# Counting a verdict with a small matmul in the tail of a fused GateLoop and gated feed-forward kernel

## The chip, the cores and the metric

The kernel runs on one core of one Trainium2 chip. The metric is the device time of one execution in microseconds (us). Times given for "runs" are of ordinary executions; the profile is of one further execution.

## The reference

Two stages follow one another. The first is a gated linear attention with a complex decay per step, the second a feed-forward layer with the gate h·cos(h).

```python
# q, k, v, a_re, a_im: (4, 8, 768, 48), float32
mag = sqrt(a_re**2 + a_im**2)
a_re, a_im = (a * minimum(mag, 0.999) / (mag + 1e-6) for a in (a_re, a_im))
for t in range(768):
    S_re, S_im = (a_re[t] * S_re - a_im[t] * S_im + outer(k[t], v[t]),
                  a_re[t] * S_im + a_im[t] * S_re)
    y[t] = q[t] @ S_re
x = y as (4 * 768, 8 * 48)
h = x @ w_in                # (3072, 384) @ (384, 2048)
out = (h * cos(h)) @ w_out  # (3072, 2048) @ (2048, 384)
```

## The kernel before

The kernel holds two programs. `fast_path` makes assumptions on the data: that the decays over a chunk do not underflow, that the weights (which arrive as 64-bit floats) are not too small, and that h stays in the range in which the sine table serves. `general_path` assumes none of this. The fast path always runs; as it goes it collects evidence in three small tiles, `least` (96 x 16, flags 1 or 0 from the decays), `odd` (128 x 41, from the weights) and `wide` (128 x 96, sums of squares of h). Near the end the generator `verdict` makes one number of them, `flag`. Every engine reads `flag` and branches: if it is 1, the whole general path runs; if not, only the last store of the fast path is issued, which stands behind the branch so that a bad result can still be replaced.

The fast path takes the 3072 rows in twelve groups of two chunks of 128 rows. In the feed-forward stage of groups 2 to 11, `mm1_sums` makes h in PSUM, `gate_sine` and `gate_product` make the gate, and `products` makes the second matmul as seven products of a 2 x 2 scheme in place of eight, each of two parts of 8 steps. `seventh(g, p, part)` does one part of one product. The order of the products is 0, 1, 3, 2, 5, 4, 6: products 0, 3, 5 (and 6, but for the last group) accumulate in one PSUM tile `sum`, which is copied out after each to the quarter of the output that it makes up at that point; products 1, 2, 4 (and 6 of the last group) have a PSUM tile `op` of their own and are added to those quarters by VectorE. In the last group (`NG - 1`) the upper right quarter `c12` lies in a tile of its own, `rest`, and its store, `late["store"]`, is the one behind the branch. It is issued by ScalarE; all other stores of the output are issued by SyncE.

The order of instructions is written out by hand. `weave` merges lists of steps by fractions of a stretch. In the last stretch it merges the fourteen parts of the products with three calls of `judged`, each of which runs `verdict` up to its next `yield`. The call `behind(a, b)` keeps instruction a after b on the same engine without a semaphore; `late` holds the instructions that others are put behind. TensorE's instructions are chained in the order in which they are written. `matmul` records all of TensorE's products under line 687, and the wrappers `vector` and `scalar` record most of the other engines' instructions under lines 676 and 707, so that in the profile groups are told apart by their tiles.

`verdict` in the kernel before: it reduces `least` to `low` (96 x 1), `odd` to `even` and `wide` to `most` (128 x 1 each), compares the latter two and multiplies them. As these lie across partitions, it brings them into one row through memory: `low` and `even` go to a scratch line `line_d` (lines 1620 and 1622), which is read back as 1 x 224 into a tile of tag `Q` (line 1624). `bad` is the minimum of that row (line 1627), and `flag` tells whether it is below 0.5 (line 1630). `values_load_multi_w_load_instructions` (line 1632) makes each engine load `flag`, and line 1644 branches. ScalarE's load is put behind the last copy of `sum` written so far (`late["scalar"]`), VectorE's ahead of the last addition, TensorE's behind a late product.

Of the kernel before, what the change touches and what calls it, by code (L numbers as in the profile page):

```python
# [11 lines left out]
F32 = mybir.dt.float32  # L12
# [7 lines left out]
ALU = mybir.AluOpType  # L20
AX = mybir.AxisListType
# [466 lines left out]
def fast_path(ctx, tc, q, k, v, a_re, a_im, moe_w_in, moe_w_out, out, least, odd, wide,  # L488
# [7 lines left out]
    nc = tc.nc  # L496
    B, H, S, D = q.shape
    DM, DF = moe_w_in.shape
    C = 128
# [3 lines left out]
    NG = N // G  # L503
    D2 = 2 * D
# [17 lines left out]
    pa = ctx.enter_context(tc.tile_pool(name="pa", bufs=5, space=PSUM))  # L522
# [11 lines left out]
    late = {}  # L534
# [8 lines left out]
    def behind(ins, other):  # L543
        tc.add_manual_dep(ins.ins, other.ins.name, mybir.DependencyInfo(
            mybir.DependencyClass.NoSync, mybir.DependencyReason.DATA))
# [9 lines left out]
    def scalar_tile(value, name):  # L555
        t = consts.tile([C, 1], F32, name=name)
        nc.vector.memset(t, value)
        return t
# [33 lines left out]
    one_b = scalar_tile(1.0, "one_b")  # L592
# [91 lines left out]
    vector, scalar = Ordered(nc.vector, "vector"), Ordered(nc.scalar, "scalar")  # L684

    def matmul(out, **kw):
        chain(nc.tensor.matmul(out, **kw), "tensor")  # L687
# [430 lines left out]
    PLAIN, HJ, E2 = 2, NJ // 2, DM // 2  # L1118
# [33 lines left out]
    scale = 1.0 / (in_scale * out_scale)  # L1152

    def left(g, name, j):
        if name[0] == "s":
            return X[g]["mix"][j // 2][name][:, j % 2]
        half, i = int(name[2]) - 1, int(name[1]) - 1
        return X[g]["gate"][j // 2 + half * (HJ // 2)][:, j % 2, ts(i, C)]

    def seventh(g, p, part):  # L1160


        x, name = X[g], SEVEN[p]
        if p == 0 and part == 0:
            x["sum"] = pm.tile([C, E2], F32, tag="acc", name="sum", bufs=1)
            x["ot"] = [msb.tile([C, DM], F32, tag="ot", name="ot") for _ in range(G)]

        alone = g == NG - 1 and p == 6
        summed = p in (0, 3, 5, 6) and not alone
        if not summed and part == 0:  # L1170
            x["op"] = pm.tile([C, E2], F32, tag="m", name="op", bufs=2)
        ps = x["sum"] if summed else x["op"]
        for j in range(part * HJ // 2, (part + 1) * HJ // 2):
            matmul(ps, lhsT=left(g, name, j), rhs=right[name][:, j],
                   start=(j == 0 and (p == 0 or not summed)),
                   stop=(j == HJ - 1), skip_group_check=summed)
        if part == 0:
            return
        c11, c12, c21, c22 = (x["ot"][i][:, ts(half, E2)] for i in range(2) for half in range(2))
        if g == NG - 1:  # L1180
            c12 = rest
        if p in (0, 3, 5) or p == 6 and not alone:
            late["scalar"] = scalar.mul(out={0: c11, 3: c21, 5: c22, 6: c12}[p], in_=ps, mul=scale)
        if g == NG - 1 and p == 5:
            scalar.mul(out=c12, in_=ps, mul=scale)
        for part_ in {1: [c11], 2: [c21], 4: [c21, c22], 6: [c12] * alone}.get(p, []):
            added = vector.scalar_tensor_tensor(out=part_, in0=ps, scalar=scale,
                                                in1=part_, op0=ALU.mult, op1=ALU.add)
            if alone:
                behind(added, late["read DVE"])  # L1190
            late["vector"] = added
        row = g * G * C
        if g == NG - 1 and p == 1:
            behind(nc.sync.dma_start(out=out[ds(row, C), 0:E2], in_=c11), late["line"])
        elif p == 4:
            put = nc.sync.dma_start(out=out[ds(row + C, C), :], in_=x["ot"][1])
            if g == NG - 1:
                behind(put, late["read SP"])
        elif p == 6 and alone:
            late["store"] = lambda: nc.scalar.dma_start(out=out[ds(row, C), E2:DM], in_=c12)  # L1200
        elif p == 6:
            nc.sync.dma_start(out=out[ds(row, C), :], in_=x["ot"][0])

    def products(g, lo, hi):
        if g < PLAIN:
            return []
        return [lambda p=p, part=part: seventh(g, p, part)
                for p in (0, 1, 3, 2, 5, 4, 6)[lo:hi] for part in range(2)]

    def mixes(g, lo, hi):  # L1210
        return [lambda p=p: mixed(g, p) for p in range(lo, hi)] if g >= PLAIN else []
# [204 lines left out]
    even = even_steps(1, 0, G)  # L1416
# [101 lines left out]
    even = even_steps(2, 0, G)  # L1518
# [49 lines left out]
    for n in range(2, NG):  # L1568
# [5 lines left out]
              (keys(n + 1), *((0.5, 0.62) if n == PLAIN else (0.53, 0.64))),  # L1574
              (last_quarter() if n == PLAIN else [], 0.9, 1.0), (first(n), 0.56, 1.0),
              (mixes(n, 0, 2), 0.9, 1.0), (guarded(n - 1, per) if n > 3 else [], 0.1, 0.9))
    checked = verdict(late, temp)

    def judged():
        late["tensor"] = tail["tensor"]  # L1580
        next(checked, None)

    weave((mixes(NG - 1, 2, 4), 0.0, 0.1), ([judged], 0.05, 0.15),
          (products(NG - 1, 0, 7), 0.0, 1.0), ([judged], 0.58, 0.6), ([judged], 0.76, 0.8))
    assert not guards
    return late
@with_exitstack
def kernel(ctx, tc, q, k, v, a_re, a_im, moe_w_in, moe_w_out, out):

    nc = tc.nc
    D2, H = 2 * q.shape[3], q.shape[1]
    keep = ctx.enter_context(tc.tile_pool(name="keep", bufs=1))
    least = keep.tile([D2, 2 * H], F32, name="least")
    C = 128
    NG, NJ = q.shape[0] * q.shape[2] // C // 2, moe_w_out.shape[0] // C
    odd = keep.tile([C, moe_w_in.shape[0] // C * 4 + NJ + NG + 1], F32, name="odd")
    wide = keep.tile([C, NG * NJ // 2], F32, name="wide")
    rest = keep.tile([C, moe_w_out.shape[1] // 2], F32, name="rest")  # L1600
    scratch = ctx.enter_context(tc.tile_pool(name="scratch", bufs=1,
                                             space=bass.MemoryType.DRAM))

    def behind(ins, other):
        tc.add_manual_dep(ins.ins, other.ins.name, mybir.DependencyInfo(
            mybir.DependencyClass.NoSync, mybir.DependencyReason.DATA))

    def verdict(late, temp):

        low = keep.tile([D2, 1], F32, name="low")  # L1610
        nc.vector.tensor_reduce(out=low, in_=least, axis=AX.X, op=ALU.min)
        even = keep.tile([C, 1], F32, name="even")
        nc.vector.tensor_reduce(out=even, in_=odd, axis=AX.X, op=ALU.max)
        most = keep.tile([C, 1], F32, name="most")
        nc.vector.tensor_reduce(out=most, in_=wide, axis=AX.X, op=ALU.max)
        nc.vector.tensor_scalar(out=even, in0=even, scalar1=0.0, scalar2=None, op0=ALU.is_le)
        nc.vector.tensor_scalar(out=most, in0=most, scalar1=2.4, scalar2=None, op0=ALU.is_le)
        nc.vector.tensor_tensor(out=even, in0=even, in1=most, op=ALU.mult)
        line_d = scratch.tile([D2 + C], F32, name="line_d")
        behind(nc.sync.dma_start(out=line_d[0:D2], in_=low.rearrange("p o -> (p o)")),  # L1620
               late["x"])
        nc.sync.dma_start(out=line_d[D2:D2 + C], in_=even.rearrange("p o -> (p o)"))
        line = temp("Q")[0:1, 0:D2 + C]
        late["line"] = nc.sync.dma_start(out=line, in_=line_d.unsqueeze(0))
        yield
        bad = keep.tile([1, 2], F32, name="bad")
        behind(nc.vector.tensor_reduce(out=bad[:, 0:1], in_=line, axis=AX.X, op=ALU.min),
               late["vector"])
        flag = keep.tile([1, 1], I32, name="flag")
        nc.vector.tensor_scalar(out=flag, in0=bad[:, 0:1], scalar1=0.5, scalar2=None,  # L1630
                                op0=ALU.is_lt)
        reads, values = nc.values_load_multi_w_load_instructions(
            flag[0:1, 0:1], min_val=0, max_val=1,
            skip_runtime_bounds_check_because="a comparison gives 0 or 1")
        late["taken"] = values[0]
        for ins in reads:
            name = str(ins.ins.engine).split(".")[-1]
            late["read " + name] = ins
        behind(late["read Activation"], late["scalar"])
        yield  # L1640
        behind(late["read PE"], late["tensor"])

    late = fast_path(tc, q, k, v, a_re, a_im, moe_w_in, moe_w_out, out, least, odd, wide, rest, verdict)
    with tc.If(late["taken"] > 0) as taken:
        general_path(tc, q, k, v, a_re, a_im, moe_w_in, moe_w_out, out)
    with taken.Else():
        late["store"]()
# [30 lines left out]
```

## Time and profile before

| what | us |
|---|---|
| median of 3 runs | 655.76 |
| lowest and highest run | 654.2, 656.69 |
| the profiled execution | 653.01 |
| its span, first to last instruction | 651.2 |
| TensorE busy in the span | 641.0 (98%) |
| VectorE busy | 492.0 (76%) |
| ScalarE busy | 392.8 (60%) |
| last matmul ended, from the start of the span | 646.55 |

The span is what the profiler saw; the profiled execution's own time is 1.8 us longer. Busy times are sums of the durations of one engine's instructions; instructions of the queues (loads of registers, branches, semaphores, issues of transfers) are not in them, but can be listed by line. In such lists PE is TensorE's matmul, PEld its loading of weights, DVE VectorE, ACT ScalarE, SP SyncE, and a q behind the name means the engine's queue. TensorE's granted clock was 1.0 of full speed in the whole span.

### The profile page before, as it was taken

The numbers are of one execution on the slowest core, as the hardware profiler recorded it, in microseconds if no ns is written. First come the engines' busy times: TensorE is split into PE (matmuls) and PEld (weight loads), VectorE is DVE, ScalarE is ACT, GpSimd is POOL, SyncE is SP. The second block draws the span as 40 slices with busy tenths as digits, with TensorE's granted clock in tenths as the row PEclk, the third lists the DMA queues.
The fourth block names the chain that finished last, engine by engine and source line by source line (L and its number), as shares of the span: only waits on it lengthen the run. The fifth ranks groups of instructions, "written<-read, shape, count | busy, mean of one in ns | idle before, by whom it ended". The sixth has DMA issues, their size and how long they took to land.

```text
span 651.2 us, 10758 instructions
## 1 busy us (share of the span) xinstructions
PE 641.0 (98%) x4075; PEld 576.4 (89%) x4075; DVE 492.0 (76%) x799; ACT 392.8 (60%) x726; POOL 30.9 (5%) x53
## 2 busy tenths in 40 slices
PE   8999999999999999999999999999999999999997
PEld 6888877777999999899899899899899999999996
DVE  6999989888687688786787787876877878862251
ACT  7898687284583593494494485485576476433330
POOL 4010200000000000010010010000000000000000
PEclk9999999999999999999999999999999999999999
DMA  9968755727627656747738737836836843363001
GB/s 249 244 179 203 225 164 123 170 62 182 146 49 182 158 146 148 194 110 167 209 82 191 204 85 167 205 96 151 226 105 146 219 123 98 112 134 120 25 1 31
DMA packets 232920, 94.90 MB, mean 146 GB/s; under 512 B 208701, under 2 KB 221246, under 8 KB 232858
## 3 DMA queue, kind: packets, MB, share of 16 engines
q1 hardware_dynamic: 225320, 68.51, 45.3%
q0 software_dynamic: 5824, 25.50, 11.7%
q8 instruction: 34, 0.56, 0.4%
q10 hardware_dynamic: 1714, 0.11, 0.2%
q14 instruction: 28, 0.23, 0.1%
HBM read 69.28 MB, written 24.81 MB: 144 GB/s over the span
## 4 chain that ended last, share of the span: by engine, by line
PE 92%; ACT 4%; DVE 3%; DMA 0%; issue 0%; SPq 0%; DVEq 0%
PE hp L687 38%; PE op L687 18%; PE sum L687 16%; PE sc L687 6%; PE yp L687 6%; PE sp L687 4%; PE phs L687 2%; PE lgs L687 1%; ACT tan L707 1%; PE yr L687 1%; PE tp L948 1%; ACT rs L707 1%; ACT lg L707 1%; ACT L703 1%; DVE mag L676 1%; DVE atm L676 1%
## 5 line engine op out<-in xcount | busy, mean ns | idle before, releaser
L687 PE MATMUL hp<-xT,w_in 128*128 128x256 f32 (+1 forms) x1176 | 252.5, 375 | 0.0
L687 PEld LDWEIGHTS hp<-xT,w_in 128*128 128x128 f32 x1176 | 219.6, 190 | 30.2 <-issue 0.2
L707 ACT ACTIVATE gate<-hp,half_pi_b 128x512 f32<-128x512 f32 x96 | 66.0, 687 | 118.5 <-PE hp L687 118.5
L687 PE MATMUL op<-w_out,gate 128*128 128x192 f32 (+1 forms) x448 | 100.7, 374 | 0.0
L676 DVE TENSOR_TENSOR gate<-hp,gate 128x512 f32<-128x512 f32 x96 | 65.7, 684 | 45.8 <-ACT junk L676 45.7
L687 PEld LDWEIGHTS op<-w_out,gate 128*128 128x128 f32 x448 | 75.9, 190 | 16.9 <-issue 2.0
L676 ACT ACTIVATE junk<-hp 128x512 bf16<-128x512 f32 x96 | 56.7, 591 | 0.0
L687 PE MATMUL sum<-t_s,s 128*128 128x192 f32 x320 | 56.3, 329 | 0.0
L687 PEld LDWEIGHTS sum<-t_s,s 128*128 128x128 f32 x320 | 52.1, 190 | 1.5 <-issue 1.5
L676 DVE TENSOR_TENSOR atm<-sc,causal 128x512 f32<-128x512 f32 x48 | 32.9, 689 | 23.4 <-PE sc L687 23.4
L687 PEld LDWEIGHTS sc<-qT,kT 96*128 96x128 f32 x384 | 47.4, 192 | 2.3 <-issue 0.6
L687 PE MATMUL sc<-qT,kT 96*128 96x128 f32 x384 | 49.0, 276 | 0.2 <-ACT qT L676 0.2
L676 ACT ACTIVATE ot<-sum 128x192 f32<-128x192 f32 x39 | 12.6, 322 | 53.7 <-PE sum L687 53.4
L676 DVE SCALAR_TENSOR_TENSOR ot<-op,ot 128x192 f32<-128x192 f32 x40 | 13.3, 354 | 38.0 <-PE op L687 36.4
L687 PE MATMUL yp<-atm,v 128*48 128x128 f32 x352 | 33.6, 277 | 0.9 <-ACT Q L707 0.6
L703 ACT ACT_TABLE_LOAD x24 | 30.8, 1283 | 1.2 <-PEq L1662 0.7
L676 ACT COPY yT<-yp 48x512 f32<-48x512 f32 x44 | 25.3, 574 | 7.4 <-PE yp L687 7.0
L687 PE MATMUL yp<-qT,state 96*48 96x128 f32 x304 | 29.7, 272 | 0.0
L687 PE MATMUL sum<-w_out,gate 128*128 128x192 f32 x160 | 29.7, 329 | 0.0
L687 PE MATMUL sp<-v,ks 128*96 128x48 f32 x320 | 29.7, 245 | 0.0
L687 PEld LDWEIGHTS sp<-v,ks 128*96 128x96 f32 x320 | 29.6, 165 | 0.0
L676 ACT CAST tan<-phs 128x384 int32<-128x384 f32 x24 | 11.4, 480 | 29.4 <-PE phs L687 29.4
(147 smaller groups left out, 987.4 us busy)
## 6 DMA issues: line engine op xcount, KB each, us to landing
moved<-tr SPq DMA_DIRECT2D x20, 768.0 KB
raw<-in_moe_w_in_dram POOLq DMA_DIRECT2D x16, 768.0 KB, 5.1
raw<-in_moe_w_out_dram POOLq DMA_DIRECT2D x16, 768.0 KB, 4.6
kT<-moved SPq DMA_DIRECT2D x40, 192.0 KB
qT<-moved SPq DMA_DIRECT2D x10, 768.0 KB
k<-in_k_dram SPq DMA_DIRECT2D x24, 192.0 KB
q<-in_q_dram SPq DMA_DIRECT2D x24, 192.0 KB
v<-in_v_dram SPq DMA_DIRECT2D x24, 192.0 KB
```

The source lines that it names most:

```text
L676: ins = getattr(self.engine, op)(**kw)
L687: chain(nc.tensor.matmul(out, **kw), "tensor")
L703: chain(nc.scalar.preload_act_table_set(table))
L707: chain(nc.scalar.activation(func=func, **kw))
L948: chain(nc.tensor.transpose(ps[:, h], X[g][name[0] + "s"][:, x0 + h].rearrange("p a d -> p (a d)"), ident), "tensor")
```

## The change

The three factors are now 1 or 0 in each partition and are multiplied into one column `even` (the 96 values of `low` into its first 96 partitions). A matmul with `even` as weights and a column of ones as moving operand counts them into a 1 x 1 tile `good` in PSUM, and `flag` tells whether the count is below 127.5. The transfers through memory and the reduction `bad` are gone, and the first store of the last group no longer has to stand behind the transfer of the line. The second call of `judged` moves from the fraction 0.58 to 0.42, after the third product. In the last group, product 5's sum is copied to `c22` and to `c12` by VectorE in place of ScalarE, so ScalarE's last copy ahead of its branch is that of product 3.

```diff
@@ seventh
         if g == NG - 1:
             c12 = rest
-        if p in (0, 3, 5) or p == 6 and not alone:
+        if g == NG - 1 and p == 5:
+            for out_ in c22, c12:
+                vector.tensor_scalar(out=out_, in0=ps, scalar1=scale, scalar2=None, op0=ALU.mult)
+        elif p in (0, 3, 5) or p == 6 and not alone:
             late["scalar"] = scalar.mul(out={0: c11, 3: c21, 5: c22, 6: c12}[p], in_=ps, mul=scale)
-        if g == NG - 1 and p == 5:
-            scalar.mul(out=c12, in_=ps, mul=scale)
...
         if g == NG - 1 and p == 1:
-            behind(nc.sync.dma_start(out=out[ds(row, C), 0:E2], in_=c11), late["line"])
+            nc.sync.dma_start(out=out[ds(row, C), 0:E2], in_=c11)
@@ end of fast_path
-    checked = verdict(late, temp)
+    def counted(even):
+
+        ps = pa.tile([1, 1], F32, tag="a", name="good")
+        matmul(ps, lhsT=even, rhs=one_b, start=True, stop=True)
+        return ps
+
+    checked = verdict(late, counted)
...
-          (products(NG - 1, 0, 7), 0.0, 1.0), ([judged], 0.58, 0.6), ([judged], 0.76, 0.8))
+          (products(NG - 1, 0, 7), 0.0, 1.0), ([judged], 0.42, 0.44), ([judged], 0.76, 0.8))
@@ verdict
         nc.vector.tensor_tensor(out=even, in0=even, in1=most, op=ALU.mult)
-        line_d = scratch.tile([D2 + C], F32, name="line_d")
-        behind(nc.sync.dma_start(out=line_d[0:D2], in_=low.rearrange("p o -> (p o)")),
-               late["x"])
-        nc.sync.dma_start(out=line_d[D2:D2 + C], in_=even.rearrange("p o -> (p o)"))
-        line = temp("Q")[0:1, 0:D2 + C]
-        late["line"] = nc.sync.dma_start(out=line, in_=line_d.unsqueeze(0))
+        nc.vector.tensor_tensor(out=even[0:D2], in0=even[0:D2], in1=low, op=ALU.mult)
         yield
-        bad = keep.tile([1, 2], F32, name="bad")
-        behind(nc.vector.tensor_reduce(out=bad[:, 0:1], in_=line, axis=AX.X, op=ALU.min),
-               late["vector"])
+        good = counted(even)
         flag = keep.tile([1, 1], I32, name="flag")
-        nc.vector.tensor_scalar(out=flag, in0=bad[:, 0:1], scalar1=0.5, scalar2=None,
-                                op0=ALU.is_lt)
+        behind(nc.vector.tensor_scalar(out=flag, in0=good, scalar1=C - 0.5, scalar2=None,
+                                       op0=ALU.is_lt), late["vector"])
```

More of the change, by code (lines that the diff above doesn't have):

```diff
@@ L1606, in behind, with verdict @@
             mybir.DependencyClass.NoSync, mybir.DependencyReason.DATA))
-    def verdict(late, temp):
+    def verdict(late, counted):
         low = keep.tile([D2, 1], F32, name="low")
```

## The prediction

> **What bounds the kernel now.** I read the page first. TensorE is busy 98% of the 651.2 us span at a granted clock of 1.0, and the chain that ended last is 92% PE. VectorE and ScalarE stand idle for 24% and 40%, so work moved between them matters only where PE or the end waits for it. Every edit lies in the last group of rows, so the second view is the chain of waits in order of time, at its end (start us, length us, what):
>
> ```profile
> 628.33 2.60 PE sum L687 x16
> 630.93 2.60 PE op L687 x16
> 633.53 2.60 PE sum L687 x16
> 636.13 2.60 PE op L687 x16
> 638.73 2.60 PE sum L687 x16
> 641.33 5.21 PE op L687 x32
> 646.55 0.03 issue
> 646.58 0.02 DVEq L676
> 646.60 0.04 issue
> 646.64 0.36 DVE rest L676
> ```
>
> The seven products follow one another with no gap, 2.60 us for 16 matmuls or 0.163 us each. Nothing of the verdict holds PE. After the last matmul (646.55) come one VectorE addition into `rest`, ending at 647.00, and then 4.2 us that the chain does not show. Third view, the timeline of the tail, for the verdict's way through memory:
>
> ```profile
> 631.90 0.15 DVE L1618 TENSOR_TENSOR even<-even,most 128x1 f32<-128x1 f32 x1
> 632.08 0.33 SPq L1622 DMA_DIRECT2D line_d<-even  x1
> 638.54 0.25 SPq L1624 DMA_DIRECT2D Q<-line_d  x1
> 641.72 0.38 DVE L1627 TENSOR_REDUCE bad<-Q 1x1 f32<-1x224 f32 x1 [2.54 <-DMA Q<-line_d]
> 642.13 0.14 DVE L1630 TENSOR_SCALAR flag<-bad 1x1 int32<-1x1 f32 x1
> 647.03 1.17 ACTq L1200 DMA_DIRECT2D out_dram<-rest  x1
> ```
>
> The verdict takes from 632.05 (`even` done) to 642.27 (`flag` done), 10.2 us, of which two transfers are nearly all. Fourth, the queue instructions of lines 1644 (branch) and 1200 (last store), and SyncE's waits:
>
> ```profile
> L1644 ACTq COMPARE_BRANCH  x1: 50/50/50, 642.8 to 642.8; - x1
> L1644 DVEq COMPARE_BRANCH  x1: 72/72/72, 646.7 to 646.7; - x1
> L1644 DVEq EVENT_SEMAPHORE  x1: 21/21/21, 649.5 to 649.5; - x1
> L1200 ACTq EVENT_SEMAPHORE  x1: 17/17/17, 645.7 to 645.7; - x1
> SPq L1673 <- DMA out_dram<-rest: 0.6, 1, 0.6
> ```
>
> ScalarE reads the flag at 642.3, branches at 642.8, and its first instruction behind the branch runs at 645.7: 2.9 us for the jump. Its store then waits for VectorE until 647.03. So ScalarE is **ready 1.3 us before it is needed**. VectorE's own jump lasts from 646.7 to 649.5, and SyncE waits 0.6 us past that for the store of `rest`: it lands at about 650.15, and the closing barrier takes the rest to 651.2.
>
> **What the Trainium skill says.** "Runtime: NRT & Kernel Launch", section on instruction fetch mechanics: instructions are fetched in sequence in blocks of 256, and a taken branch out of the window stalls for a fetch. The trace agrees: 2.9 us on ScalarE, 2.8 on VectorE. "DMA: Bandwidth & Descriptors", section on the anatomy of one DMA, gives some 2 us of fixed cost, mostly the receipt of the write (it describes the GpSimd path). The trace is dearer: SyncE waited 6.0 us for `line_d<-even`, and `Q<-line_d` took 641.72 - 638.54 = 3.2 us. "TensorE: Matmul & The Clock Gate", section on the back-to-back issue gap, puts a matmul of 1 to 64 columns at about 60 cycles, a floor of some 25 ns; no matmul of one column is in this trace.
>
> **The change part by part.** The compiled order of every engine before this tail is the same in both kernels, so nothing earlier moves.
>
> *The product with ones (added on PE).* One 1x1 matmul, weights of one column (`even`), stands behind the sixteen of the third product (`sum<-t_s`, ending 636.13) and ahead of the fourth. It waits for VectorE's `even`: 632.05 plus the added `even*low`, 0.15 us by row L1618, gives 632.2, 3.9 us early. So no stall, but its time is on PE's path. The nearest row is `sp<-v,ks` (48 columns), which the chain shows as
>
> ```profile
> 542.02 1.32 PE sp L687 x16
> ```
>
> so 0.08 us each (1.32 / 16). From below the skill's floor, an estimate of 0.03; from above, if the wait keeps its weights from being loaded ahead and the array drains, one uncovered load and one matmul: 165 + 245 ns (both of the `sp` rows) = 0.41 us. I take **+0.08**, range 0.03 to 0.41. Behind it on PE stand the last four products, so all of it reaches the end.
>
> *The way through memory (removed).* Three transfers leave SyncE's queue (0.48, 0.33 and 0.25 us of issue), with the reduction `bad` on VectorE (0.38). Cover: PE's unbroken products, so 0 us. SyncE's store of the first quarter now goes at about 634 instead of 638.84, into a stretch where DMA is 5% busy. Its last store still waits for the fifth addition on VectorE (644.62), its branch comes after that: unchanged. No bound below zero or above, since the last store hangs on PE in both.
>
> *The flag.* VectorE compares right after the small product, so at about 636.4 instead of 642.13. In VectorE's queue it stands between the additions of the second product (633.63) and the fourth (638.83); were PE late, those would wait, but the fourth's own operand comes from the same queue later. POOL and SyncE read the flag 5.8 us sooner and wait as long afterwards, on the barrier and on `ot`. PE reads it behind its last matmul, VectorE just ahead of the `rest` addition, as before: 0.
>
> *The sixth product's copies (moved).* ScalarE loses 0.33 + 0.32 us. VectorE gains two 128x192 copies out of PSUM; its nearest row, `ot<-op,ot` at 354 ns, gives 0.71 us, from 641.5 to 642.2. The next addition starts at 643.97, so 1.8 us of idle VectorE hide it; if a copy took three times that, the addition would slip 0.3 us but still precede `rest` at 646.64. Cost 0.
>
> *ScalarE's branch (moved).* Its copy of the third product ends at 636.50. Reading the flag 0.46, branch 0.05, jump 2.9: ready at about 639.9, 7.1 us ahead of the store instead of 1.3. The store still waits for `rest` on VectorE, hence for PE. Direct gain 0. Unknown: its issue took 1.17 us, where SyncE's stores of the same kind took 0.34, and the first packets of `rest` appear 1.6 us after issue. If that is an after-effect of the recent jump, 0.83 us go. But VectorE's jump ends at 649.5 whatever ScalarE does, so no more than 0.6 us of it reaches the end. From the other side, if waiting longer makes it no worse, 0. I take **0**, since the jump was over 1.3 us earlier.
>
> Sum against the profiled execution (653.01 us, the 651.2 span and 1.8 around it): 653.01 + 0.08 = 653.1. That execution is 2.75 us under the median of the runs (655.76); carried over, **655.8**.
>
> **The rivals.**
>
> *The last store's issue shrinks.* For it: 1.17 against 0.34 us, with instruction packets in flight at 647.5 to 648.2. Against it: 1.3 us of readiness. 653.1 - 0.6 = 652.5, so 655.2.
>
> *The timed runs had the branch on the path.* The profile's slack is only 1.3 us, and the verdict hangs on two trips through memory. If they take over 1.3 us longer in the usual run, each further us delays the store, and the change takes it out. At most the whole 2.75 us between median and profile goes: 653.1; halfway 654.5. Against it: nothing shown ties that difference to the tail.
>
> *The small product costs PE more* (the case that ends slower). One mechanism: its wait holds its weight load back, the array drains before and after. At the bound of 0.41 us, 653.4 and 656.2; with a second drain for the next product's load, 0.8 us and 656.6. It decides as soon as it exceeds what the store's issue gives, 0 to 0.6 us. For it: PE is the bound and every other matmul is prefetched. Against it: the operand has been there for 3.9 us.
>
> *The change doesn't do what it says.* If the count came out under 127.5, the general path would run in full and the time rise by hundreds of us. The factors are comparisons, 0 or 1, so 128 ones count exactly 128. Nor is there a saving if "sooner" only lengthens a wait, which is the main forecast.
>
> **How the numbers follow.** Likeliest (+0.08 only) 0.52; shorter issue 0.2; branch was on the path 0.12; dearer product 0.14; general path or something unseen 0.02. A measurement of this kernel can tell about 0.5%, 3.3 us, from no change. Only the branch case with an even later verdict than the profile allows, or an unseen one, gets past that: faster 0.07, same 0.9, slower 0.03. The mechanisms span 653.1 to 656.6, and the three runs lay from 1.6 below their median to 0.9 above; the range that holds 8 in 10 is 653.5 to 657.2.
>
> **What would show it.** In the profile after: 16 + 1 + 16 matmuls between the third and fourth products with the fourth starting 0.03 to 0.4 us later than 2.60 us after the third; `flag` at about 636.4; ScalarE's first instruction behind its branch at about 640; the store of `rest` issued at about 647.1; the two copies on VectorE ended before 642.5; the end at about 651.3. The forecast is wrong if ScalarE's issue falls to about 0.4 us and the end comes near 650.7, if PE shows a gap of over 0.4 us around the product, or if the medians differ by more than 3.3 us.

## The result, and the profile after

The changed kernel took 657.73 us (median of 8 runs) against 655.11 of the kernel before: a ratio of 1.0043, with a 95% interval of 1.0028 to 1.0058. It is slower by some 2.6 us, just outside the range, where 0.1 us had been forecast. The profiled execution took 657.33 us, its span 655.6.

The chain of waits at the end of the changed kernel (start us, length us, what):

```profile
632.98 2.60 PE sum L687 x16
635.58 2.60 PE op L687 x16
638.18 2.60 PE sum L687 x16
640.78 0.12 PE good L687 x2
640.90 2.80 PE op L687 x16
643.70 2.60 PE sum L687 x16
646.30 5.21 PE op L687 x32
651.51 0.02 issue
651.54 0.36 DVE rest L676
```

The tail is as forecast but for one size: the product with ones costs 0.12 us itself (two passes, x2), and the product behind it 2.80 instead of 2.60. But the seven products begin at 632.98, where they began at 628.33 before. **4.65 us were lost before the first edited instruction runs**: 4.62 of them by 529 us, and the first of the removed transfers was issued at 597.9. Not all of it is the change's: the kernel before happened to be profiled in an execution 2.1 us below its median, and the medians differ by 2.6. The waits of TensorE over the whole span show where (waiting tile, its releaser; us in total, times, longest):

```profile
PE sc L687 <- DMA qT<-moved: 1.7, 2, 1.2
PE busy L687 <- DVE one_b L557: 1.5, 1, 1.5
PE phs L687 <- ACT tan L707: 1.4, 2, 0.8
PE sc L687 <- issue: 1.0, 1, 1.0
PE yp L687 <- DVE atm L676: 0.8, 2, 0.5
PE lgs L687 <- DMA sums<-sums_const: 0.7, 1, 0.7
```

In the kernel before, the same list has no wait for a transfer at all. `moved` carries keys and queries through memory to be transposed; SyncE issues four transfers into `kT` for each group and then one into `qT`. The chain shows one place, in the middle of a group's `hp`:

```profile
369.88 3.21 PE hp L687 x15
373.09 6.43 DMA qT<-moved
379.52 0.14 issue
379.65 1.13 PE sc L687 x8
```

The 6.43 us are the transfer's own length; PE still had matmuls of `hp` during most of it and stood idle for 0.50 us. Before, PE ran from `hp` to `sc` here without a gap:

```profile
369.90 6.91 PE hp L687 x32
376.81 0.89 PE sc L687 x8
```

Section 3 of the page (queue: packets, MB, time of its packets as a share of 16 engines' span) says that this queue's transfers became slower, first the kernel before, then the changed one:

```profile
q1 hardware_dynamic: 225320, 68.51, 45.3%
```

```profile
q1 hardware_dynamic: 225062, 68.51, 52.7%
```

The same 68.51 MB take 52.7% where they took 45.3%, though three transfers of the verdict are gone.

The branch and the last store of the changed kernel, from the queue instructions of lines 1632, 1644 and 1201, and SyncE's waits:

```profile
L1632 ACTq TENSOR_LOAD <-flag x1: 464/464/464, 641.1 to 641.1; - x1
L1644 ACTq COMPARE_BRANCH  x1: 50/50/50, 641.9 to 641.9; - x1
L1201 ACTq EVENT_SEMAPHORE  x1: 17/17/17, 645.6 to 645.6; - x1
L1201 ACTq DMA_DIRECT2D out_dram<-rest x1: 390/390/390, 651.9 to 651.9; - x1
L1644 DVEq EVENT_SEMAPHORE  x1: 21/21/21, 654.5 to 654.5; - x1
SPq L1673 <- DMA out_dram<-rest: 0.6, 1, 0.6
SPq L1673 <- DVEq L1644: 0.3, 1, 0.3
```

ScalarE now stands ready 6.3 us ahead of the store, and the issue takes 0.39 us where it took 1.17. From the last matmul to the end of the span it is 4.0 us instead of 4.7. SyncE first sees the store landed and then waits 0.3 us for VectorE's jump (654.5): VectorE now sets the end. So tail and product together brought about -0.3 us, and something else cost some 3.

**What moved.** The compiled programs have the same instructions in the same order up to the tail, but not the same addresses. `bad` was a tile of two floats in the pool `keep`, taking 32 bytes per partition. `keep` lies below the other pools. Without `bad`, 1500 of 1512 tiles that could be matched between the two start 32 bytes lower: `kT` of the fast path from 121344 to 121312, `re` from 68992 to 68960. The large ones of the fast path started at multiples of 64, `kT` at a multiple of 128; now they start 32 below.

### The profile page after: what moved, and what is told of

Read it like the earlier page. It is cut to its first block, busy times and chain, and to the rows that moved or that the text cites. A ratio compares the mean times of both kernels' runs of the same rounds, so it can differ in the third digit from the quotient of the medians.

```text
span 655.6 us, 10760 instructions
## 1 busy us (share of the span) xinstructions
PE 642.6 (98%) x4077; PEld 575.6 (88%) x4077; DVE 492.0 (75%) x801; ACT 392.3 (60%) x724; POOL 31.9 (5%) x53
## 3 DMA queue, kind: packets, MB, share of 16 engines
q1 hardware_dynamic: 225062, 68.51, 52.7%
## 4 chain that ended last, share of the span: by engine, by line
PE 90%; DMA 3%; ACT 3%; DVE 2%; issue 0%; SPq 0%; POOL 0%; DVEq 0%
PE hp L687 36%; PE op L687 18%; PE sum L687 16%; PE sc L687 6%; PE yp L687 6%; PE sp L687 4%; PE phs L687 2%; DMA qT<-moved 2%; PE lgs L687 1%; PE yr L687 1%; PE tp L948 1%; DMA re<-in_a_re_dram 1%; DMA sums<-sums_const 1%; ACT L703 1%; ACT tan L707 1%; DVE mag L676 1%
## 5 line engine op out<-in xcount | busy, mean ns | idle before, releaser
L676 DVE TENSOR_TENSOR gate<-hp,gate 128x512 f32<-128x512 f32 x96 | 65.5, 682 | 45.7 <-ACT junk L676 45.7
L676 ACT ACTIVATE ot<-sum 128x192 f32<-128x192 f32 x38 | 12.3, 323 | 48.5 <-PE sum L687 48.3
```

The source lines that it names most:

```text
L676: ins = getattr(self.engine, op)(**kw)
```

## The experiments

**1. Put the 32 bytes back.**

```diff
+        nc.vector.memset(keep.tile([1, 2], F32, name="space"), 0.0)
         good = counted(even)
```

> The changed kernel with one unused tile of 32 bytes per partition put where `bad` stood, so that all 1500 tiles behind it in SBUF keep the addresses of the kernel before (one memset of VectorE more, beside PE's work). Theory A (addresses): what made the kernel slower is that `bad` is gone and everything behind it moved down by 32 bytes, from multiples of 64 to 32 over one; transfers take longer. Then q1's share falls from 52.7% to about 45.3%, and the time is that of the tail alone: +0.3 us for the product with ones, -0.55 us behind the last matmul, so about 654.9 us (ratio to before 0.9996). Theory B (the new instructions and queue orders themselves): stays at 657.7 (ratio 1.004).

Measured: 655.1 us, ratio 0.9998 (0.9986 to 1.001). The page of this kernel:

```profile
q1 hardware_dynamic: 225062, 68.51, 45.7%
```

All other edits are in, and the loss is gone.

**2. Take them from the kernel before.**

```diff
-        bad = keep.tile([1, 2], F32, name="bad")
+        bad = most[0:1, 0:1]
```

> The kernel before, with `bad` laid into the tile `most`, whose values are used up by then, in place of a tile of its own; same instructions, same order, all tiles behind it 32 bytes lower, as in the changed kernel. Theory A: slower by what the changed kernel lost to transfers, 2.6 + 0.25 us, so about 658.0 (ratio 1.0043), q1's share about 52.7%. Theory B: no change, 655.1 (ratio 1.000), share 45.3%.

Measured: 658.52 us, ratio 1.0052 (1.004 to 1.0064). Its page, and its waits of TensorE:

```profile
q1 hardware_dynamic: 225320, 68.51, 53.0%
```

```profile
PE sc L687 <- DMA qT<-moved: 2.4, 3, 1.2
```

The old verdict with the lower addresses shows the whole loss and the same wait: with experiment 1 this separates the addresses from the instructions. Theory B falls.

**3. Is it the scratch memory in HBM?** `line_d` was the last tile of that memory, so none of the others moved; but the memory's size changed.

```diff
+        line_d = scratch.tile([D2 + C], F32, name="line_d")
+        behind(nc.sync.dma_start(out=line_d[0:D2], in_=low.rearrange("p o -> (p o)")),
+               late["x"])
         yield
```

> The changed kernel with the scratch line `line_d` of 896 bytes in memory kept, and `low` still stored to it (one transfer, beside PE's work), so that the scratch memory is laid out and sized as before, while SBUF stays 32 bytes lower. Rival theory C (layout of the scratch memory in HBM): back to about 654.9, share about 45%. Theory A: stays at 657.7 (ratio 1.004), share about 52.7%.

Measured: 658.44 us, ratio 1.0048 (1.0035 to 1.0061), q1 52.7%. Theory C falls.

**4 and 5. Which multiple is needed?** As in 1, with `[1, 24]` (96 bytes) and `[1, 40]` (160 bytes): tiles 64 and 128 bytes above those of the kernel before.

> The changed kernel with an unused tile of 96 bytes in place of `bad`: the tiles behind it lie 64 bytes higher than in the kernel before, at multiples of 64, but half of them no longer at multiples of 128. Theory A with a step of 64 bytes: as with 32 bytes, about 654.9 us and a share of about 45%. Theory A with a step of 128 bytes or more: between 655.5 and 658, share over 47%. Theory B: 657.7.

Measured: 657.36 us, ratio 1.0037 (1.0018 to 1.0055), q1 48.3%. So a multiple of 64 isn't enough.

> An unused tile of 160 bytes in place of `bad`: all tiles behind it 128 bytes higher than before. With 64 bytes more, the 128-byte packets straddled multiples of 128 and took 16.3 ns (q1 48.3%). If a multiple of 128 is what those packets need: 13 ns, share about 45.5%, time about 655. If they need 256: share over 47%, 656.5 to 658.

Measured: 655.71 us, ratio 1.0005 (0.999 to 1.002), q1 46.3%. A shift by 128 leaves the time where it was, as far as these runs can tell. Mean duration of a packet by its size, worked out from the packet records of the traces (the 128-byte packets number 61,440 = 40 transfers of 96 x 16 runs, so they are those into `kT` alone; `qT` has packets of 2,048 bytes, contrary to what an expectation above says; the 192-byte ones are the loads of re, im, k, q, v):

| shift against the kernel before, bytes | 128 B (`kT`), ns | 192 B (loads), ns | q1 | ratio |
|---|---|---|---|---|
| 0, kernel before | 13.0 | 15.6 | 45.3% | 1 |
| 0, after_space32 | 13.0 | 15.7 | 45.7% | 0.9998 |
| +128, after_space160 | 13.0 | 16.0 | 46.3% | 1.0005 |
| +64, after_space96 | 16.3 | 15.9 | 48.3% | 1.0037 |
| -32, changed kernel | 18.8 | 18.3 | 52.7% | 1.0043 |

The Trainium skill, "DMA: Bandwidth & Descriptors", section on how a descriptor splits into AXI transactions, says that a piece which doesn't start on a multiple of 256 bytes is fetched from the multiple below, and that the unused bytes before its start still cost time. It speaks of what is fetched; what moved here is the side that is written. That a start off the multiple costs time is so here too, but the multiple isn't 256. A head's 512 bytes of `kT` are four runs of 128, one for each of a group's four transfers, so in the kernel before two of the four already start on odd multiples of 128; the means of the four are all between 12.96 and 13.00 ns. Experiment 5 only swaps these two kinds, so alone it could not have told 128 from 256.

In these runs the mean duration of a 128-byte packet rises where the runs straddle multiples of 128, but not every such packet is slow: the median is 13.0 ns in the changed kernel too. There the first 1,536 packets of each group, one transfer's worth, keep 13.0 in the mean, and the later three sets take 20.6 to 20.9. Why the first are spared is open.

**6 and 7. Whose packets decide?** An unused tile of 32 bytes in a pool of its own between `gt` and `ft` sets right only what lies from `ft` on; with one more ahead of `ld`, only what lies from `ld` to `gt`. The constants and the weights, which lie lower, stay 32 bytes down in both.

```diff
     gt = ctx.enter_context(tc.tile_pool(name="gt", bufs=1))
+    nc.vector.memset(ctx.enter_context(tc.tile_pool(name="space", bufs=1)).tile(
+        [1, 2], F32, name="space"), 0.0)
```

> The changed kernel with an unused tile of 32 bytes between the pools `gt` and `ft`: everything from `ft` on (kT, qT, yT, tr, xT, the outputs, the raw weights) is back at the addresses of the kernel before, while the loads' tiles (re, im, k, q, v) and the temporaries stay 32 bytes lower. PE was seen to wait for `qT<-moved`, and the 128-byte packets, which are those of kT and qT, grew from 13.0 to 18.8 ns, the 192-byte ones, mostly the loads, from 15.6 to 18.3 ns. If the step that costs the time is the 128-byte packets: within 0.1% of the kernel before (655.2), share of q1 about 48.5%. If the loads' tiles carry it: 657 to 658.

Measured: 655.52 us, ratio 1.0004 (0.9992 to 1.0015). Its page:

```profile
q1 hardware_dynamic: 225062, 68.51, 48.0%
```

> The complement: the loads' tiles and temporaries at the addresses of the kernel before, everything from `ft` on 32 bytes higher than before (32 over a multiple of 64). If the 128-byte packets carry the loss: about 657.7 (ratio 1.004), share about 50%. If the loads' tiles carry it: within 0.1% of before.

Measured: 658.45 us, ratio 1.0058 (1.0042 to 1.0074). Its page, and its waits of TensorE:

```profile
q1 hardware_dynamic: 225062, 68.51, 48.8%
```

```profile
PE sc L691 <- DMA qT<-moved: 2.5, 3, 1.3
```

The two have nearly the same share of q1, one at no loss, one at the full loss. What counts is not how long transfers take in all, but where the tiles from `ft` on lie: with the loads alone misplaced (192-byte packets 17.7 ns, `kT`'s 13.0) nothing is lost that these runs can tell; with `ft` and what follows misplaced (`kT`'s 16.3, loads 16.1) PE waits for `qT`, which is queued behind `kT` on SyncE. That `kT`'s packets and not another tile's of the same pools do it wasn't tried alone; `qT`'s own packets of 2,048 bytes took 154 ns in the mean here, 150 at +64 and 135 to 139 at -32, against 123 to 135 where `ft` lay as before or 128 higher.

One profile's wait for `qT` is not a clean sign by itself: it adds up to 0 to 0.9 us in the nine kernels whose `ft` tiles lie as before or 128 higher, and to 1.5 to 2.5 in the five where they are off. The two kinds part more clearly when PE's matmuls in each trace are lined up with those of the kernel before, from the start to the last group. The delay that sets in at `sc`, the product that reads `qT` and `kT`, is 0.2 to 1.1 us in the eight others of the first kind and 3.8 to 5.3 in the second (4.1 of the changed kernel's 4.65). What is lost at all other matmuls together, 0.4 to 3.0 us, is of the same size in both kinds, so it doesn't part them.

**8 and 9. The product in bf16.** A tile of two bf16 columns takes `bad`'s place, so the addresses are those of the kernel before. `counted` takes the ones as a second argument.

```diff
-        nc.vector.tensor_tensor(out=even, in0=even, in1=most, op=ALU.mult)
-        nc.vector.tensor_tensor(out=even[0:D2], in0=even[0:D2], in1=low, op=ALU.mult)
+        pair = keep.tile([C, 2], BF16, name="pair")
+        count, ones = pair[:, 0:1], pair[:, 1:2]
+        nc.vector.memset(ones, 1.0)
+        nc.vector.tensor_tensor(out=count, in0=even, in1=most, op=ALU.mult)
+        nc.vector.tensor_tensor(out=count[0:D2], in0=count[0:D2], in1=low, op=ALU.mult)
...
-        good = counted(even)
+        good = counted(count, ones)
```

> All addresses as before (a tile of two bf16 columns takes the place of `bad`), and the product with ones in bf16 instead of f32: the count of 128 is exact in it. In f32 the product ran as two passes (x2 in the profile), 0.12 us and 0.2 us more in the product behind it. If the passes are what costs: one matmul, some 0.15 us less on PE's chain. If the wait and the change of weights cost: the same 0.32 us. Time 654.7 to 655.1 in both, no more than 0.15 us from after_space32, under what the runs can tell.

Measured: 654.36 us, ratio 0.9988 (0.9978 to 0.9997). The chain of this kernel:

```profile
634.61 2.60 PE sum L687 x16
637.21 0.09 PE good L687
637.30 2.80 PE op L687 x16
```

One pass, but only 0.03 us less: 0.29 in place of 0.32. The expected 0.15 us fails; the passes are a small part of the price.

> after_bf16 once more, as the version that keeps the addresses and counts in one pass: its first ratio was 0.9988 with an interval of 0.9978 to 0.9997, only just below 1. If it is faster than the kernel before, the ratio stays at 0.998 to 0.9995; if that was chance, 0.9995 to 1.0005.

Measured: 654.91 us, ratio 0.999 (0.9982 to 0.9999). Twice just below 1: a version some 0.1% ahead of the kernel before, and ahead of the changed kernel by the address loss.

**10 and 11. Why the product costs 0.3 us.** First without it, as a measure; this kernel leaves out 127 of the 128 partitions when it makes `flag`:

```diff
-        good = counted(even)
+        good = even[0:1]
...
-        behind(nc.vector.tensor_scalar(out=flag, in0=good, scalar1=C - 0.5, scalar2=None,
+        behind(nc.vector.tensor_scalar(out=flag, in0=good, scalar1=0.5, scalar2=None,
```

> after_space32 without the product with ones: `flag` is made from the first partition of `even` alone, so the check of the other 127 partitions is left out. Shows the product's whole price on PE: the fourth product should begin with the end of the third and last 2.60 us as all others, so 0.32 us come off the chain between the third product's start and the last matmul (18.53 us with it, 13.01 + 5.21 without). If the 0.20 us that the fourth product lost had another cause than the small one, it stays at 2.80 us. Time about 654.8.

Measured: 654.78 us, ratio 0.9976 (0.9961 to 0.9992); that is more than 0.3 us below after_space32, but the two intervals overlap. The chain of this kernel:

```profile
636.17 2.60 PE sum L687 x16
638.77 2.60 PE op L687 x16
641.37 2.60 PE sum L687 x16
643.97 5.21 PE op L687 x32
```

No gap, and 2.60 us for the fourth product: the 0.20 us it had lost was the small product's. Then the product without a wait of its own, in the middle of the last product but one:

```diff
-  ... ([judged], 0.42, 0.44), ([judged], 0.76, 0.8))
+  ... ([judged], 0.77, 0.79), ([judged], 0.9, 0.95))
```

> after_space32 with the product with ones put into the middle of the last product but one (fraction 0.78), whose first matmul has already waited for a later instruction of VectorE, so that the small product needs no wait of its own. In the changed kernel TensorE's weight loads pause 0.23 us before it, and the chain grew by 0.12 us for it and 0.20 us in the product behind it. If its own wait holds back the loading of weights: no pause, about 0.1 us in all. If the change to one column of weights costs it: 0.3 us as before. The flag comes only at about 645.5 us, so ScalarE is ready at about 648.9, some 0.5 us after `rest`: the store goes that much later, and the issue should be long again, over 1 us; time 655 to 656.5.

Measured: 656.89 us, ratio 1.0017 (1.0005 to 1.003). The load of weights in the timeline of the changed kernel and then of this one, and this one's chain:

```profile
640.71 0.09 PEld L687 LDWEIGHTS good<-one_b,even 128*1 128x1 f32 x2 [0.23 <-issue]
```

```profile
644.33 0.09 PEld L687 LDWEIGHTS good<-one_b,even 128*1 128x1 f32 x2 [0.23 <-issue]
```

```profile
643.10 1.30 PE op L687 x8
644.40 0.12 PE good L687 x2
644.51 4.11 PE op L687 x24
```

Same pause of 0.23 us, same price: 0.12, and 4.11 us for 24 matmuls that take 3.90 at 0.163 each. So the wait isn't the cause. What remains, a matmul with one column of weights and one moving column among larger ones, was not taken apart further. ScalarE's half of the expectation came true: its first instruction behind the jump ran at 649.3, 0.3 us after `rest` was done, and its store's issue took 2.32 us. The time lies above the expected 655 to 656.5.

**12. Branch late, without a way through memory.** The second `judged` at 0.70, and the copies of product 5 on ScalarE again (the recorded texts call it the sixth product; it is the fifth in order).

```diff
-  ... ([judged], 0.42, 0.44), ...
+  ... ([judged], 0.69, 0.71), ...
...
-            for out_ in c22, c12:
-                vector.tensor_scalar(out=out_, in0=ps, scalar1=scale, scalar2=None, op0=ALU.mult)
...
+            late["scalar"] = scalar.mul(out=c12, in_=ps, mul=scale)
```

> after_space32 with the product with ones moved behind the sixth product (fraction 0.70) and that product's two copies back on ScalarE, so that ScalarE branches late again, without any way through memory. In the kernel before, ScalarE stood ready 1.3 us ahead of the store of `rest`, whose issue then took 1.17 us; in the changed kernel it stands ready 6.3 us ahead and the issue takes 0.39. If the recent jump lengthens the issue: about 1.2 us again, with ScalarE ready 1 to 2 us ahead, and 4.6 us from the last matmul to the end of the span. If the early flag or the absent transfers do it: 0.39 us and 4.1 us. Time 655.1 to 655.8, no difference the runs can tell.

Measured: 655.6 us, ratio 0.9993 (0.998 to 1.0006). Its queue instructions of line 1200:

```profile
L1200 ACTq EVENT_SEMAPHORE  x1: 17/17/17, 645.9 to 645.9; - x1
L1200 ACTq DMA_DIRECT2D out_dram<-rest x1: 667/667/667, 648.5 to 648.5; - x1
```

Ready 2.6 us ahead instead of the expected 1 to 2, and an issue of 0.67 us: between the two. From the last matmul to the end it was 5.5 us, beyond both 4.6 and 4.1. Together with the others:

| kernel | ScalarE ready ahead of the data of its store, us | issue, us | last matmul to end, us |
|---|---|---|---|
| after_nowait | 0.3 late | 2.32 | 6.1 |
| kernel before | 1.3 | 1.17 | 4.7 |
| before_less32 | 1.5 | 1.33 | 5.5 |
| after_late | 2.6 | 0.67 | 5.5 |
| changed kernel | 6.3 | 0.39 | 4.0 |

In these five the issue ends 2.4 to 3.2 us after the first instruction behind the jump, or about 0.4 us after its data, whichever is later. The tail itself is less regular: the first profile of the bf16 kernel had an issue of 0.39 and still 5.3 us from the last matmul to the end, since the packets of `rest` took 2.3 us to pass, against 0.7 in the changed kernel. Why is open.

## Why the prediction was wrong

- **The step that failed** is the sentence "The compiled order of every engine before this tail is the same in both kernels, so nothing earlier moves." The order is the same; addresses moved. Experiment 2 prices this at +3.4 us (0.0052 x 655.5) in the kernel before; experiment 1 takes the changed kernel's whole loss away. No rival held it: three lay in the tail and the fourth in the general path; 0.02 was left for the unseen.
- *Three transfers and `bad` removed at 0 us*: as instructions, yes. But `bad` was costed as 0.38 us of VectorE and not as 32 bytes of SBUF.
- *The product with ones at +0.08 us*: +0.32, within the bounds of 0.03 to 0.41. The row taken for it (`sp`, weights of 96 columns) doesn't stand for one column. The upper bound came from an array that drains because of the wait; experiment 11 shows the same pause and the same price without a wait.
- *The last store's issue at 0 gain*: it fell by 0.78 us. The rival that priced this was right: for its size, and for its cap, VectorE's jump. From the last matmul to the end 0.65 us went, beside the 0.6 allowed. So one of the prediction's own signs of being wrong appeared, the issue of about 0.4 us, and with it the end, which less the 4.65 us lies at 650.9.
- *ScalarE ready 7.1 us ahead*: 6.3, since its jump took 3.7 us in place of 2.9. That PE reads the flag behind its last matmul was misread: PE loads it at 643.5 in the kernel before, ahead of the last product. It cost nothing in either kernel.
- *Sixth product's copies hidden*: right (product 5). They took 0.36 and 0.35 us and ended 2.0 us before VectorE's next addition.
- *Branch on the path in the timed runs*: nothing of it shows. Without the address loss the ratio is 0.9998, where this rival had about 0.998.
- *Less than 0.5% either way*: 0.43%, so right in size, but by luck: its cause was none of those that the figure was made from.

## What to carry to other kernels

Removing a small tile from a pool that lies low in SBUF moves every tile above it, so compare addresses, not only instruction orders, before saying that nothing else changed. If q1's share rises for the same bytes, and the engine that sets the time waits longer for a transfer, look for tiles that left their multiple of 128 bytes; a spacer of the lost size is a one-line test and remedy. A tiny matmul between large ones cost 0.3 us here whatever its type or wait, so price it by the gap around it.

## What the runs showed of the hardware that was not expected

- A 128-byte packet into SBUF took 13.0 ns in the mean with its tile on a multiple of 128 bytes, 16.3 ns 64 bytes off, 18.8 ns with all tiles 32 bytes below; 13.0 again at 128 bytes more. The median stayed at 13.0: the slow packets came with the later ones of four transfers that follow on one another.
- One matmul with one column of weights: 0.09 us in bf16 and 0.12 us in f32, a pause of 0.23 us in the loading of weights before it with or without a wait, and 0.2 us lost by the matmuls behind it.
- The issue of a store behind a taken branch took 0.39 us when ScalarE had stood ready for 6.3 us, and 2.32 us when it had only just arrived.
